# Copying a transposed tile out of PSUM in runs: which side of the copy hops

## The chip, the cores and the metric

The kernel runs on one core of one Trainium2 chip. The metric is device time in microseconds (us) of one execution; the kernel before takes 200.59 us (median of three executions, 200.13 to 200.97). The core's engines each work through their own queue in order: TensorE (PE in the profile, with its weight loads listed as PEld), VectorE (DVE), ScalarE (ACT), GpSimd (POOL) and SyncE (SP, which here issues the DMAs). TensorE writes its results into PSUM; ScalarE and VectorE carry them from PSUM into SBUF, from where TensorE reads its operands.

## The reference

The input is a batch of 8 sequences of 2496 rows with 256 features. It is Fourier transformed over rows and over features and the real part kept; the result, 19968 rows of 256, goes through a soft mixture of experts with 32 slots, 8 experts of 4 slots each.

```python
X = np.fft.fft(np.fft.fft(x, axis=1), axis=2).real      # 8 x 2496 x 256, then 19968 x 256
logits = X @ phi                                        # 19968 x 32
d = exp(logits - logits.max(0)); d /= d.sum(0) + 1e-9   # over all rows, for each slot
slot_input = d.T @ X                                    # 32 x 256
h = np.maximum(slot_input[e] @ w1[e], 0); slot_out[e] = h @ w2[e]   # for each expert e
c = exp(logits - logits.max(1)); c /= c.sum(1) + 1e-9   # over the slots, for each row
out = c @ slot_out                                      # 19968 x 256
```

## The kernel before, in words

The transform is never formed as a whole. Only the logits need it, so the projection on the 32 slots is folded into the feature transform, and the row transform, of length 2496 = 64 x 39, is done as a 64-point and a 39-point transform on the much smaller projected data. The batch of 8 is worked as 4 pairs of sequences (index `p`). For each pair the kernel goes through parts, which a written-out list (`ORDER`) strings together; the scheduler of the language then places the instructions of all engines, with the parts of two or three pairs interleaved.

- `part_a` (L210, twice to three times per pair): VectorE adds and subtracts mirrored rows of the loaded `x` into `eo` tiles (L222 to L227); TensorE transposes them 128 x 128 at a time into `pt` (L231); ScalarE copies these to `et` (L232); TensorE multiplies with the folded projection into `z` (L238); ScalarE copies `z` to `zs` (L246).
- `part_t` (L252): TensorE transposes the ten 128 x 128 blocks of `zs` into three PSUM banks (L259), and ScalarE copies them to the SBUF tile `zt` (L262, L266). This is where the change is.
- `part_b` (L268): TensorE does the 64-point transform with `zt` as its weights, three slots at a time, into `a` (L275); ScalarE copies to `o1` (L282).
- `part_c`, `part_e`, `part_d`, `part_u`: the 39-point transform (`lp`, `lm`, L293 and L294) gives the logits `lt`; column maxima (`mx`, `mt`, `nm`), exponentials on ScalarE (`d`, L316), and the inverse transform back (`e` L331, `d` L348, `ds` L356, `u` L373) to the slot inputs.

After the fourth pair come the sum over pairs (`part_m`), the two expert layers (L472, L492) and, for each pair, the row softmax (`part_s`) and the output product (`po`, L576, copied out at L580 and stored). About 22 to 101 us is the stretch in which `part_a`, `part_t` and `part_b` of the pairs lie.

The tile `zt` of a pair has 128 partitions, and in each the shape `[33, 2, 20]`: 33 places (the 32 slots and one of padding), for each place two halves of 20 coefficients. It is fp32, so a place is 40 numbers, 160 bytes. The transposes leave a bank the other way round: `(c s)`, 16 coefficients of 32 slots each, slots next to each other. So the copy also turns slots and coefficients round, and either its reading or its writing has to hop. Two banks of 512 columns go to `zt[:, :, 0, 0:16]` and `zt[:, :, 1, 0:16]`; of the third, two pieces of 128 columns go to the coefficients 16 to 19 of both halves. Per pair that is two copies of 128x512 and two of 128x128, 16 copies in all.

What stands around them in ScalarE's queue matters for the reading. For the second pair (`p` = 1) it is, as the kernel's program has it (each row: line, operation, output<-input, shape; `et_2_0` and `et_2_1` are the last two `et` tiles of that pair, `zs` its last `z` copy):

```order
L262 COPY zt_530<-zt_0_532 128x16x32
L262 COPY zt_530<-zt_1_538 128x16x32
L232 COPY et_2_0_499<-pt_4_0_504 128x512
L232 COPY et_2_1_500<-pt_4_1_510 128x512
L246 COPY zs_294<-z_2_516 128x2x2x64
L232 COPY et_0_0_555<-pt_0_0_560 128x8x64
L266 COPY zt_530<-zt_2_544 128x4x32 x2
L232 COPY et_0_1_556<-pt_0_1_566 128x8x64
```

On TensorE the same stretch is as follows (`pt_4_*` are the last transposes of the pair, `z_2` its last projection, `zt_2` its third bank, `pt_0_*` the first transposes of the next pair):

```order
L231 MATMUL pt_4_0_504<-cs_70,eo_4_293 128x128 x4
L231 MATMUL pt_4_1_510<-cs_70,eo_4_293 128x128 x4
L238 MATMUL z_2_516<-et_2_0_499,wphi 32x128 x4
L238 MATMUL z_2_516<-et_2_1_500,wphi 32x128 x8
L306 MATMUL mt_1_442<-cs_70,mx_1_440 5x120
L311 MATMUL mt_0_415<-cs_70,mex_0_418 120x6
L231 MATMUL pt_0_0_560<-cs_70,eo_0_549 128x128 x4
L259 MATMUL zt_2_544<-cs_70,zs_294 128x128 x2
L231 MATMUL pt_0_1_566<-cs_70,eo_0_549 128x128 x4
L275 MATMUL a_0_687<-cs_72,zt_530 120x128 x4
```

So `z_2` waits for the `et` copies, which stand behind the two copies of L262, and `a` waits for the copies of L266.

Of the kernel before, what the change touches and what calls it, by code (L numbers as in the profile page):

```python
# [17 lines left out]
NSLOT = 32  # L18
# [98 lines left out]
def _build(nc, tc, xh, phih, w1h, w2h, cins, where, out, out0):  # L117
    from contextlib import ExitStack, nullcontext

    v, sc, pe = nc.vector, nc.scalar, nc.tensor  # L120
    ctx = ExitStack()
    with ctx:
# [12 lines left out]
        def sa(shape, name, dt=F32):  # L135
            return sb.tile(shape, dt, name=name, tag="sa", bufs=2)
# [7 lines left out]
        def bank(name, dt=F32):  # L144
            return pp.tile([128, 512], dt, name=name, tag="ps")
# [39 lines left out]
        ps = bank("psphi")  # L185
# [22 lines left out]
        zs, zt, o1, dpm, esb, dsb = {}, {}, {}, {}, {}, {}  # L208
# [43 lines left out]
        def part_t(p):  # L252
            zt[p] = sa([128, GS * NG, 2, NKC], f"zt{p}")
            nc.gpsimd.memset(zt[p][:, NSLOT:], 0.0)
            for b, units in enumerate(([(0, q) for q in range(4)], [(1, q) for q in range(4)], [(0, 4), (1, 4)])):
                ps = bank(f"zt{p}_{b}")
                for i, (h, q) in enumerate(units):
                    u, nq = q // 2, 2 if q < 4 else 1
                    pe.transpose(ps[:, i * 128 : i * 128 + 128], zs[p][:, 4 * u + nq * h + q % 2], ident)  # L259
                if b < 2:  # L260
                    dst = zt[p][:, :NSLOT, b, 0:16].rearrange("p s c -> p c s")
                    sc.copy(dst, ps.rearrange("p (c s) -> p c s", s=NSLOT))  # L262
                else:
                    for h in range(2):
                        dst = zt[p][:, :NSLOT, h, 16:20].rearrange("p s c -> p c s")
                        sc.copy(dst, ps[:, h * 128 : h * 128 + 128].rearrange("p (c s) -> p c s", s=NSLOT))  # L266

        def part_b(p):  # L268
            o1[p] = sa([120, 2, NG, NA], f"o1{p}")
# [323 lines left out]
        def after(f, *a):  # L593
# [5 lines left out]

        parts = {  # L600
            "a": part_a, "t": lambda p, _: part_t(p), "b": lambda p, _: part_b(p), "c": part_c,
            "e": part_e, "d": part_d, "u": lambda p, _: part_u(p), "w": lambda *_: load_w(),
            "m": lambda *_: part_m(), "l": lambda i, _: part_l(i), "v": lambda i, _: part_v(i),
# [54 lines left out]
```

## Time and profile before

| | |
|---|---|
| median of three executions | 200.59 us (200.13 to 200.97) |
| the profiled execution | 201.22 us, of it the span shown in the profile 199.4 us |
| TensorE busy | 174.7 us (88% of the span) |
| ScalarE busy | 132.4 us (66%) |
| VectorE busy | 131.8 us (66%) |
| L262, copies of 128x512 | 8, mean 1202 ns, 8.7 us busy |
| L266, copies of 128x128 | 8, mean 453 ns, 2.7 us busy |
| mean granted TensorE clock | 0.979 |

Times in the profile are microseconds from the start of the span unless marked ns. Two neighbouring instructions on an engine may overlap a little, so a group's busy time can be less than its count times its mean. An engine's idle time is put down to what ended it; idle time of an engine on which nothing waits costs nothing. The view of stretches gives, for each stretch, the busy time of each engine with the number of instructions that began in it, then the TensorE clock that was granted (1.00 is full speed), the share of DMA and the GB/s moved.

### The profile page before, as it was taken

How to read it: one execution, taken by the hardware profiler on the slowest of the kernel's cores; microseconds unless marked ns; L12 is line 12 of the kernel's file. 1: busy time of each engine (PE TensorE's matmuls, PEld its weight loads, DVE VectorE, ACT ScalarE, POOL GpSimd, SP SyncE). 2: the span in 40 equal slices, each digit the busy share in tenths (PEclk: the TensorE clock that was granted, in tenths of full speed). 3: DMA queues.
4: the chain of work that ended last, by engine and by line, in shares of the span. 5: the costliest groups of instructions: out<-in, count | busy, mean ns of one | idle time of the engine just before them, and what ended most of it. 6: DMA issues, size and time to landing. Idle time of an engine off the chain costs nothing.

```text
span 199.4 us, 4290 instructions
## 1 busy us (share of the span) xinstructions
PE 174.7 (88%) x1690; PEld 125.6 (63%) x1690; DVE 131.8 (66%) x238; ACT 132.4 (66%) x277; POOL 24.6 (12%) x27
## 2 busy tenths in 40 slices
PE   0499889969999999989999989999999999989900
PEld 0375575549666877556865859346788877768700
DVE  0599856989993991742357624796677888976700
ACT  2135775579876795687856963763867988896610
POOL 0000000000000000000000100767101357320000
PEclk9999999997999999999999999999999999999995
DMA  5999999998880499600393687991099999799996
GB/s 183 409 427 410 422 420 420 419 391 291 301 363 21 112 358 424 263 0 0 111 283 138 205 326 234 364 404 58 2 378 355 419 409 389 306 421 363 430 426 214
DMA packets 10707, 59.17 MB, mean 297 GB/s; under 512 B 1344, under 2 KB 1728, under 8 KB 5696
## 3 DMA queue, kind: packets, MB, share of 16 engines
q1 hardware_dynamic: 10688, 58.91, 76.0%
q8 instruction: 13, 0.21, 0.4%
q14 instruction: 6, 0.05, 0.1%
HBM read 38.46 MB, written 20.45 MB: 295 GB/s over the span
## 4 chain that ended last, share of the span: by engine, by line
PE 75%; ACT 10%; DMA 2%; DVE 2%; issue 2%; POOL 2%; SPq 0%; ACTq 0%; DVEq 0%; POOLq 0%
PE po L576 17%; PE pt L231 9%; PE z L238 7%; PE a L275 6%; PE e L331 6%; PE u L373 5%; PE d L348 4%; PE h L472 4%; PE so L492 3%; PE lp L293 3%; PE lm L294 3%; PE cT L529 2%; DMA x<-xh 2%; ACT zt L262 2%; PE lT L569 2%
## 5 line engine op out<-in xcount | busy, mean ns | idle before, releaser
L576 PE MATMUL po<-rh,lTs 128*128 128x512 f32 x160 | 42.4, 405 | 1.5 <-ACT lTs L570 0.7
L231 PE MATMUL pt<-cs,eo 128*128 128x128 f32 x160 | 26.9, 300 | 8.9 <-DVE eo L226 7.9
L576 PEld LDWEIGHTS po<-rh,lTs 128*128 128x128 f32 x160 | 28.1, 188 | 8.5 <-ACT o L580 1.8
L232 ACT COPY et<-pt 128x512 f32<-128x512 f32 x40 | 23.1, 592 | 13.8 <-PE pt L231 13.2
L580 DVE COPY o<-po 128x512 f32<-128x512 f32 (+1 forms) x40 | 26.9, 686 | 7.9 <-PE po L576 7.0
L231 PEld LDWEIGHTS pt<-cs,eo 128*128 128x128 f32 x160 | 19.9, 153 | 15.9 <-DVE eo L226 7.9
L580 ACT COPY o<-po 128x512 f32<-128x512 f32 x40 | 23.2, 595 | 7.3 <-PE po L576 7.1
L224 DVE TENSOR_TENSOR x<-x 128x1024 f32<-128x1024 f32 x16 | 19.5, 1217 | 3.0 <-DMA x<-xh 3.0
L238 PE MATMUL z<-et,wphi 128*32 128x256 f32 (+1 forms) x288 | 19.0, 371 | 1.9 <-ACT et L232 1.8
L544 POOL TENSOR_TENSOR c<-c,cm 128x640 f32<-128x640 f32 x8 | 11.8, 1489 | 28.0 <-DVE cm L543 27.0
L316 ACT ACTIVATE d<-lt,nm 120x128 f32<-120x128 f32 x44 | 13.6, 390 | 1.9 <-DVE nm L313 1.8
L226 DVE TENSOR_TENSOR eo<-x 128x512 f32<-128x512 f32 x20 | 13.6, 682 | 0.6 <-PE u L373 0.3
L238 PEld LDWEIGHTS z<-et,wphi 128*32 128x32 f32 x288 | 7.8, 113 | 9.4 <-ACT et L232 4.2
L227 DVE TENSOR_TENSOR eo<-x 128x512 f32<-128x512 f32 x20 | 13.6, 680 | 0.0
L331 PE MATMUL e<-cs,dpm 120*64 120x120 f32 x176 | 13.5, 273 | 0.0
L331 PEld LDWEIGHTS e<-cs,dpm 120*64 120x64 f32 x176 | 10.7, 136 | 3.5 <-issue 2.4
L356 ACT COPY ds<-d 64x320 f32<-64x320 f32 x24 | 10.0, 421 | 4.2 <-PE d L348 3.5
L275 PE MATMUL a<-cs,zt 128*120 128x128 f32 x88 | 12.2, 292 | 0.4 <-ACT zt L266 0.3
L275 PEld LDWEIGHTS a<-cs,zt 128*120 128x120 f32 x88 | 11.1, 196 | 1.9 <-ACT zt L266 1.3
L549 POOL TENSOR_TENSOR c<-c,cm 128x640 f32<-128x640 f32 x8 | 11.0, 1391 | 10.0 <-DVE cm L548 5.5
L570 ACT CAST lTs<-lT 128x512 fp32r<-128x512 f32 x20 | 11.5, 599 | 0.9 <-PE lT L569 0.9
L373 PE MATMUL u<-eo,ds 128*32 128x129 f32 x320 | 11.6, 275 | 0.0
(99 smaller groups left out, 251.4 us busy)
## 6 DMA issues: line engine op xcount, KB each, us to landing
x<-xh SPq DMA_DIRECT2D x16, 1024.0 KB, 11.3
out<-o SPq DMA_DIRECT2D x15, 1024.0 KB, 5.6
w<-w1h SPq DMA_DIRECT2D x6, 1024.0 KB, 8.6
w<-w2h SPq DMA_DIRECT2D x12, 512.0 KB, 6.0
x<-xh SPq DMA_DIRECT2D x4, 896.0 KB, 10.3
out<-o SPq DMA_DIRECT2D x4, 768.0 KB, 6.0
w<-w1h SPq DMA_DIRECT2D x4, 512.0 KB, 5.2
w<-w2h SPq DMA_DIRECT2D x2, 1024.0 KB, 8.0
```

The lines of the kernel that those rows point to most:

```text
L224: v.tensor_tensor(x[:, 0:4], x[:, 0:4], x[:, 4:8], op=ALU.add)
L226: v.tensor_tensor(e[:, :, 0:128], x[:, 0:4, 0:128], x[:, 0:4, 128:256], op=ALU.add)
L227: v.tensor_tensor(e[:, :, 128:256], x[:, 0:4, 0:128], x[:, 0:4, 128:256], op=ALU.subtract)
L231: pe.transpose(b[:, g * 128 : g * 128 + 128], e[:, g, k * 128 : k * 128 + 128], ident)
L232: sc.copy(tr[k][:, :, :, qi, :], b.rearrange("p (g h a) -> p g h a", g=4, h=2))
L238: pe.matmul(z[32 * g : 32 * g + 32, o : o + n], wphi[:, w, :], tr[k][:, g].rearrange("p h q a -> p (h q a)"), start=i != 1, stop=i != 0, t ...
L275: pe.matmul(ps[:120, i * 128 : i * 128 + 128], zt[p][:, GS * g : GS * g + GS].rearrange("p s h c -> p (s h c)"), C("wa"), start=True, stop ...
L316: sc.activation(d[:, g], L[:, g], AF.Exp, bias=nm[:, g : g + 1], scale=1.0)
L331: pe.matmul(ps[64 * k : 64 * k + 64, 120 * i : 120 * i + 120], dpm[p, hf][:, k, 3 * j + i, :], C(name), start=True, stop=True, tile_positi ...
L373: last = pe.matmul(ub[32 * g : 32 * g + 32, 0:129], dsb[p][:, k, c, :], e[:, 0:129] if k == 0 else e[:, 127:256], start=cc == 0, stop=cc == 9,
L576: pe.matmul(po, lT[:, i, :], rh[j].rearrange("p k d -> p (k d)"), start=j == 0, stop=j == 1,)
L580: (v.tensor_copy if n_ev[0] % 2 else sc.copy)(ot[:np_, 2 * i : 2 * i + 2, :].rearrange("p k d -> p (k d)"), po[:np_])
```

## The change

Both sides of the copies of L262 and L266 are described the other way round. Before, the copy goes through the numbers coefficient by coefficient: it reads PSUM in one piece and writes each number 160 bytes after the one before. Afterwards it goes place by place: it reads numbers that lie 32 apart in PSUM (128 bytes), and writes 16 numbers next to each other (64 bytes; 4 numbers, 16 bytes, in the smaller copies), then hops 160 bytes to the next place. The same numbers go to the same addresses, in as many instructions.

```diff
                 if b < 2:
-                    dst = zt[p][:, :NSLOT, b, 0:16].rearrange("p s c -> p c s")
-                    sc.copy(dst, ps.rearrange("p (c s) -> p c s", s=NSLOT))
+                    sc.copy(zt[p][:, :NSLOT, b, 0:16], ps.rearrange("p (c s) -> p s c", s=NSLOT))
                 else:
                     for h in range(2):
-                        dst = zt[p][:, :NSLOT, h, 16:20].rearrange("p s c -> p c s")
-                        sc.copy(dst, ps[:, h * 128 : h * 128 + 128].rearrange("p (c s) -> p c s", s=NSLOT))
+                        sc.copy(zt[p][:, :NSLOT, h, 16:20], ps[:, h * 128 : h * 128 + 128].rearrange("p (c s) -> p s c", s=NSLOT))
```

No engine's order of instructions differs; only the shapes of these copies do. In ScalarE's queue the rows shown above now read as follows (lines at and below the edit have moved up by one or two):

```order
L261 COPY zt_530<-zt_0_532 128x32x16
L261 COPY zt_530<-zt_1_538 128x32x16
L232 COPY et_2_0_499<-pt_4_0_504 128x512
L232 COPY et_2_1_500<-pt_4_1_510 128x512
L246 COPY zs_294<-z_2_516 128x2x2x64
L232 COPY et_0_0_555<-pt_0_0_560 128x8x64
L264 COPY zt_530<-zt_2_544 128x32x4 x2
L232 COPY et_0_1_556<-pt_0_1_566 128x8x64
```

The inner count of the copies went from 32 places to 16 or 4 coefficients; what stands before and behind them is the same.

## The prediction

> **What bounds the kernel now.** First the page: busy times, and the shares of the chain that ended last.
>
> ```profile
> PE 174.7 (88%) x1690; PEld 125.6 (63%) x1690; DVE 131.8 (66%) x238; ACT 132.4 (66%) x277; POOL 24.6 (12%) x27
> PE 75%; ACT 10%; DMA 2%; DVE 2%; issue 2%; POOL 2%; SPq 0%; ACTq 0%; DVEq 0%; POOLq 0%
> ```
>
> TensorE (PE) sets the end; 10% of the chain, 20 us, is ScalarE (ACT). A faster ScalarE copy is worth only what TensorE waits for it. So next: the copies of ScalarE by shape, for what one costs (count | busy us, mean ns of one | idle before).
>
> ```profile
> L262 ACT COPY zt<-zt 128x512 f32<-128x512 f32 x8 | 8.7, 1202 | 0.6 <-PE zt L259 0.6
> L232 ACT COPY et<-pt 128x512 f32<-128x512 f32 x40 | 23.1, 592 | 13.8 <-PE pt L231 13.2
> L266 ACT COPY zt<-zt 128x128 f32<-128x128 f32 x8 | 2.7, 453 | 0.1
> L382 ACT COPY usb<-u 128x129 f32<-128x129 f32 x3 | 0.8, 257 | 0.5 <-PE u L373 0.5
> L356 ACT COPY ds<-d 64x320 f32<-64x320 f32 x24 | 10.0, 421 | 4.2 <-PE d L348 3.5 <-DVE ds L356 0.5
> L295 ACT COPY lt<-lp 120x320 f32<-120x320 f32 x4 | 1.8, 452 | 3.1 <-PE lp L293 3.1
> L534 ACT COPY c<-cT 128x480 f32<-128x480 f32 x8 | 4.4, 565 | 3.8 <-PE cT L529 3.8
> ```
>
> L262 takes twice as long as L232, which moves as many numbers; L266 takes 1.8 times L382.
>
> Then the timeline of both engines where the four pairs meet these copies (start, us, engine line; in brackets the idle time before and what ended it). The first pair:
>
> ```profile
> 22.85 2.17 ACT L262 COPY zt<-zt 128x512 f32<-128x512 f32 x2
> 24.77 0.45 ACT L246 COPY zs<-z 128x256 f32<-128x256 f32 x1
> 25.75 0.66 ACT L266 COPY zt<-zt 128x128 f32<-128x128 f32 x2
> 22.64 1.01 PE L238 MATMUL z<-et,wphi 128*32 128x128 f32 x24
> 25.28 0.44 PE L259 MATMUL zt<-cs,zs 128*128 128x128 f32 x2 [1.04 <-ACT zs L246]
> 25.55 0.60 PE L231 MATMUL pt<-cs,eo 128*128 128x128 f32 x4
> 26.46 2.73 PE L275 MATMUL a<-cs,zt 128*120 128x128 f32 x22 [0.31 <-ACT zt L266]
> ```
>
> z was done at 22.64 + 1.01 = 23.65, but its copy stood behind the two of L262 until 24.77, and TensorE stood still for 1.04 us, then 0.31 us for L266. The second pair:
>
> ```profile
> 39.62 2.16 ACT L262 COPY zt<-zt 128x512 f32<-128x512 f32 x2 [0.58 <-PE zt L259]
> 41.55 1.14 ACT L232 COPY et<-pt 128x512 f32<-128x512 f32 x2
> 40.24 0.38 PE L231 MATMUL pt<-cs,eo 128*128 128x128 f32 x2
> 42.26 1.13 PE L238 MATMUL z<-et,wphi 128*32 128x128 f32 x24 [1.64 <-ACT et L232]
> ```
>
> Here the et copies queue behind L262, and TensorE is idle for 1.64 us from 40.62. This gap has a second price, in the view of stretches (PE busy with its count, PEld, DVE, ACT, POOL, then the granted clock, DMA share, GB/s), cut in pieces of 3.41 us:
>
> ```profile
> 23.84:27.25 3.41, 2.06 (x17) 1.58 (x16) 2.16 (x4) 2.95 (x7) 0.00 (x0) 1.00 1.00 413
> 27.25:30.66 3.41, 3.41 (x29) 3.09 (x28) 1.69 (x3) 2.55 (x5) 0.13 (x1) 1.00 1.00 417
> 40.90:44.32 3.42, 2.00 (x31) 1.41 (x32) 2.92 (x6) 2.16 (x4) 0.00 (x0) 0.97 0.99 380
> 44.32:47.73 3.41, 3.40 (x17) 2.99 (x16) 3.37 (x6) 3.13 (x10) 0.00 (x0) 0.53 0.85 284
> 47.73:51.14 3.41, 3.41 (x29) 2.71 (x31) 3.02 (x5) 2.85 (x8) 0.13 (x1) 1.00 0.89 329
> ```
>
> Right behind the piece with the gap (2.00 us busy) the clock is 0.53 for one piece, and 17 matmuls begin in it where 29 do in the pieces like it. The first pair's piece, 2.06 us busy, was followed by no drop: we are at the edge.
>
> **The change part by part.** It removes and adds no instruction and moves none; 16 copies of ScalarE get another shape.
>
> *The 128x512 copies.* The new form hops on the reading side (128 bytes) and writes runs of 64. L356 reads numbers 80 bytes apart and writes runs of 16, and takes 421 ns for 320 against 452 for L295, which reads straight. L534 reads 160 bytes apart and writes runs of 12, at 565 ns for 480, between 452 at 320 and 592 at 512. Neither pays for hops in PSUM, so I take L232's 592 ns, saving 610 ns each. The ends: 421 x 512 / 320 is more than 592, so nothing shows a copy below it; above, 1202 ns (no gain) if a hop of 128 bytes reads as slowly as one of 160 writes. I take the low end because both hopping readers lie there.
>
> [...]
>
> *The 128x128 copies.* Their runs are only 4 numbers, which no row shows. The ends are L382's 257 ns and today's 453; I take 257, since a run of 12 (L534) costs nothing visible. With a pair overlapping, 0.66 us becomes about 0.40.
>
> *What a pair of copies frees.* A pair of L262 holds ScalarE from 22.85 to 24.77, 1.92 us. Pairs of copies like L232 show how closely these follow each other:
>
> ```profile
> 49.09 1.08 ACT L232 COPY et<-pt 128x512 f32<-128x512 f32 x2
> ```
>
> 1.08 less 0.59 for the last is 0.49 from start to start, so two take 0.98 and what follows may begin 0.94 us earlier. ScalarE's busy time falls by some 16 x 0.3 = 5 us; most of it is idle time elsewhere.
>
> *First pair.* The copy of zs may start at 23.83 (z is done at 23.65), TensorE's transposes at 24.34 instead of 25.28: 0.94. Then L266 starts 0.94 earlier and ends 0.26 sooner yet, at 25.18; TensorE is through L231 at 25.2 and starts a at about 25.25 instead of 26.46. **1.2 us.**
>
> *Second pair.* et starts at 40.6 instead of 41.55 (TensorE's pt is done at 40.62, so it is there in time), z at 41.3. **0.95 us.**
>
> *Third and fourth pair.*
>
> ```profile
> 64.88 2.19 ACT L262 COPY zt<-zt 128x512 f32<-128x512 f32 x2
> 66.82 0.46 ACT L246 COPY zs<-z 128x256 f32<-128x256 f32 x1
> 68.83 0.38 PE L259 MATMUL zt<-cs,zs 128*128 128x128 f32 x2
> 90.48 0.85 PE L238 MATMUL z<-et,wphi 128*32 128x128 f32 x20
> 90.55 0.79 ACT L340 COPY e<-e 128x360 f32<-128x360 f32 x2
> 91.39 1.34 PE L348 MATMUL d<-e,cs 128*128 128x320 f32 x4
> ```
>
> In the third, zs is done at 67.28 and TensorE wants it at 68.83, having been busy with other matmuls: nothing. In the fourth the e copies behind L262 release L348 at 91.39, but TensorE is in z until 90.48 + 0.85 = 91.33: nothing, and perhaps 0.1 at the a behind L266. What hides these is the interleaved work of other pairs; without it each would be another 0.95.
>
> *The half-speed piece.* With the second gap 0.95 us shorter, its piece is busy for about 2.95 us instead of 2.00, well above the 2.06 that went without a drop. Then the 12 missing matmuls fit: 12 / 29 x 3.41 = 1.4 us. Not all arrives, because VectorE (DVE) can follow only so far. Its waits there:
>
> ```profile
> 43.62 0.27 DVE L308 TENSOR_REDUCE mall<-mt 5x3 f32<-5x120 f32 x1 [0.50 <-PE mt L306]
> 48.12 0.56 DVE L318 TENSOR_TENSOR dpm<-d 120x384 f32<-120x384 f32 x1 [0.43 <-ACT d L316]
> 54.31 0.49 DVE L319 TENSOR_TENSOR dpm<-d 120x320 f32<-120x320 f32 x1
> 57.09 0.62 PE L331 MATMUL e<-cs,dpm 120*64 120x120 f32 x4
> 62.22 0.48 DVE L356 COPY ds<-d 64x320 f32<-64x320 f32 x1 [2.37 <-PE d L348]
> ```
>
> It has 0.50 + 0.43 = 0.93 us of waits to give up before 55, so its dpm, done at 54.80, comes no earlier than 53.87. TensorE needs it at 57.09 and can come forward by 3.2, against 1.2 + 0.95 + 1.4 = 3.55. By 62.22 VectorE waits for TensorE again, and later work follows. So of the 1.4 I count **1.0**.
>
> [...]
>
> *Sum.* 1.2 + 0.95 + 0.1 + 1.0 = 3.25 us off the profiled execution's 201.22 (span 199.4, 1.8 around it), 198.0. That execution lies 0.6 above the median, 200.59. Whether the runs behind the median had the half-speed piece isn't known: if so, 200.59 - 3.25 = 197.3; if not, 200.59 - 2.25 = 198.3. I take **197.9 us**.
>
> **The rivals.**
> - *Queue time alone.* The clock drops anyway (another gap falls into one window) or hadn't dropped in the runs behind the median: 2.25 us, 198.3 to 199.0. For it: at 2.00 and 2.06 us the same kernel did and didn't drop. Against: no gap of that size is left.
> - *VectorE holds the gain.* It is busy 3.37 of 3.41 us in the half-speed piece. If TensorE hangs on it more closely than I read (through the eo tiles for pt, say), 0.93 us is all that comes through: 199.7. Against: the 2.3 us between dpm and its use.
> - *The copy doesn't get cheaper.* A number read 128 bytes from the last costs what one written 160 bytes away does, and the copy stays at 1.2 us: 200.6. Against: L356 and L534. For: neither hops by a power of two. [...]
> - *Slower.* The same place, worse: the hopping read costs more than the hopping write did. From a start-to-start of 0.96 us upward every 0.1 costs 0.2 at the first, second and fourth pair, and the first pair's piece, 0.06 us from the edge, drops its clock too, 1.4. At 1.2 us: 6 x 0.24 + 1.4 = 2.8, 203.4. Nothing in the profile speaks for it beyond the stride that no row has.
>
> **How the numbers follow.** Chances: my forecast 0.45, queue time alone 0.25, VectorE 0.14, no cheaper 0.09, slower 0.07. The range runs from 196.8 (the 197.3 above with another 0.5 us from the 0.4 not counted and the two later pairs) to 200.3, which leaves out the slower and most of the no-cheaper case. 0.5%, 1.0 us, is what the timing can tell apart, so faster means below 199.6: the first two cases less 0.02, and 0.04 of the third, 0.72; within it 0.21; slower 0.07.
>
> **What would show it.** The 128x512 copies at about 590 ns and the 128x128 ones at about 260; the first pair's a at about 25.2; TensorE's wait for et in the second pair at 0.7 us or less; 29 matmuls and clock 1.00 after it; third and fourth pair with no shorter gaps on TensorE. Copies that stay above 900 ns would make it wrong at its root; copies at 590 ns with a time above 199.6, in the step from queue to TensorE.

## The result and the profile after

The changed kernel takes 197.71 us (median), against 200.36 us for the kernel before in the same comparison: a ratio of 0.9865, 95% interval 0.9835 to 0.9895, or 2.65 us less. A second comparison gave 197.48 against 200.70, 0.9835 (0.9809 to 0.9862). One of the six executions of the changed kernel took 903.28 us, for a reason that nothing here shows; the median counts it, the ratio does not, and the other five lie between 197.51 and 197.97. The profiled execution took 197.51 us with a span of 195.7, where the one before took 201.22 with 199.4.

First, the copies by shape in the changed kernel (count | busy us, mean ns of one | idle before); the lines of the edit are now L261 and L264.

```profile
L261 ACT COPY zt<-zt 128x512 f32<-128x512 f32 x8 | 4.3, 596 | 0.6 <-PE zt L259 0.6
L264 ACT COPY zt<-zt 128x128 f32<-128x128 f32 x8 | 1.8, 280 | 0.0
L232 ACT COPY et<-pt 128x512 f32<-128x512 f32 x40 | 23.0, 594 | 13.8 <-PE pt L231 13.2
```

The large copies went from 1202 to 596 ns and now cost what L232 costs, 594, the small ones from 453 to 280. Reading PSUM in hops of 128 bytes costs ScalarE nothing that can be seen here. ScalarE as a whole went from 132.4 to 127.4 us busy, 5.0 us less; the time fell by about half of that in the median.

The first pair in the timeline of ScalarE and TensorE (start, us, engine line, then idle time before):

```profile
22.72 1.08 ACT L261 COPY zt<-zt 128x512 f32<-128x512 f32 x2
23.67 0.41 ACT L246 COPY zs<-z 128x256 f32<-128x256 f32 x1
24.68 0.44 ACT L264 COPY zt<-zt 128x128 f32<-128x128 f32 x2
22.51 1.01 PE L238 MATMUL z<-et,wphi 128*32 128x128 f32 x24
24.13 0.44 PE L259 MATMUL zt<-cs,zs 128*128 128x128 f32 x2
25.17 2.72 PE L273 MATMUL a<-cs,zt 128*120 128x128 f32 x22 [0.17 <-ACT zt L264]
```

The copy of zs starts at 23.67, 0.15 us after its z is done (22.51 + 1.01) where it had been 1.12, and TensorE's wait of 1.04 us is gone; a starts at 25.17 instead of 26.46. The second pair:

```profile
38.34 1.07 ACT L261 COPY zt<-zt 128x512 f32<-128x512 f32 x2 [0.58 <-PE zt L259]
39.30 1.10 ACT L232 COPY et<-pt 128x512 f32<-128x512 f32 x2
39.95 1.14 PE L238 MATMUL z<-et,wphi 128*32 128x128 f32 x24 [0.62 <-ACT et L232]
43.09 2.01 PE L273 MATMUL a<-cs,zt 128*120 128x128 f32 x16 [0.41 <-ACT zt L264]
```

TensorE's wait for et fell from 1.64 to 0.62 us. There is also a wait that was not there before: a waits 0.41 us for the small copies.

Now the pieces of 3.41 us around the gap (PE busy with its count, PEld, DVE, ACT, POOL, granted clock, DMA share, GB/s). The clock of the profiled execution before fell at 44.13 and rose at 47.54, 0.19 us ahead of where the prediction cut its pieces. In its clock records full clock begins at 16.82, and the clock changes 27.31, 3.41 and 146.77 us from one to the next, 8, 1 and 43 times 3.41; after the change it begins at 16.96 and changes once, 174.08 us or 51 times 3.41 later. So the pieces are laid out in steps of 3.41 us from the beginning of these records. Before:

```profile
40.71:44.13 3.42, 1.81 (x30) 1.22 (x31) 2.92 (x7) 2.35 (x5) 0.00 (x0) 1.00 1.01 387
44.13:47.54 3.41, 3.40 (x17) 2.99 (x16) 3.41 (x6) 2.94 (x9) 0.00 (x0) 0.50 0.89 303
```

After the change:

```profile
37.44:40.85 3.41, 2.39 (x37) 1.82 (x36) 3.41 (x7) 2.37 (x5) 0.00 (x0) 1.00 0.99 408
40.85:44.27 3.42, 3.01 (x34) 2.47 (x23) 3.42 (x6) 2.53 (x8) 0.00 (x0) 1.00 1.02 418
44.27:47.68 3.41, 3.41 (x29) 2.65 (x31) 3.41 (x7) 3.31 (x9) 0.13 (x1) 1.00 0.98 371
```

The gap, which now ends at 39.95, lies in the first of these, with 2.39 us of work. The clock stays at 1.00, and in the third, at nearly the same time of the span as the half-speed piece before, 29 matmuls begin where there were 17. Following the same matmul through both traces shows where the 3.7 us of the span came from:

| matmul of TensorE | start before | start after | earlier by |
|---|---|---|---|
| the first transposes, pt | 7.89 | 7.65 | 0.24 |
| first pair, a | 26.46 | 25.17 | 1.29 |
| second pair, last z | 42.26 | 39.95 | 2.31 |
| second pair, a | 45.67 | 43.09 | 2.58 |
| second pair, first lp | 50.18 | 46.79 | 3.39 |
| third pair, a | 71.01 | 67.61 | 3.40 |
| fourth-pair stretch, d | 91.39 | 87.87 | 3.52 |
| fourth pair, a | 93.82 | 90.16 | 3.66 |
| first expert layer, h | 125.33 | 121.66 | 3.67 |
| last po | 189.19 | 185.56 | 3.63 |

Just ahead of the first pair's copies (22.85 to 22.72) the two executions were 0.13 us apart, which has nothing to do with the change. So: 1.16 at the first pair, 1.02 at the second pair's gap, 1.08 between that gap and lp, where the clock had been halved, nothing from 47 us to the fourth pair, 0.26 around the fourth pair, and nothing given back in the 100 us behind it.

### The profile page after: what moved, and what is told of

Read it like the earlier page. It is cut to its first block, busy times and chain, and to the rows that moved or that the text cites. A ratio compares the mean times of both kernels' runs of the same rounds, so it can differ in the third digit from the quotient of the medians.

```text
span 195.7 us, 4290 instructions
## 1 busy us (share of the span) xinstructions
PE 173.1 (88%) x1690; PEld 124.3 (63%) x1690; DVE 131.5 (67%) x238; ACT 127.4 (65%) x277; POOL 24.6 (13%) x27
## 4 chain that ended last, share of the span: by engine, by line
PE 79%; ACT 8%; DVE 3%; DMA 2%; POOL 2%; issue 2%; SPq 0%; ACTq 0%; DVEq 0%; POOLq 0%
PE po L574 17%; PE pt L231 10%; PE z L238 8%; PE e L329 7%; PE a L273 6%; PE u L371 6%; PE d L346 4%; PE h L470 4%; PE so L490 4%; PE lp L291 3%; PE lm L292 3%; PE cT L527 3%; DMA x<-xh 2%; PE lT L567 2%; POOL c L542 2%; ACT et L232 2%
## 5 line engine op out<-in xcount | busy, mean ns | idle before, releaser
L231 PE MATMUL pt<-cs,eo 128*128 128x128 f32 x160 | 26.4, 297 | 8.7 <-DVE eo L226 7.6
L232 ACT COPY et<-pt 128x512 f32<-128x512 f32 x40 | 23.0, 594 | 13.8 <-PE pt L231 13.2
L273 PE MATMUL a<-cs,zt 128*120 128x128 f32 x88 | 11.4, 279 | 0.6 <-ACT zt L264 0.6
L273 PEld LDWEIGHTS a<-cs,zt 128*120 128x120 f32 x88 | 10.2, 183 | 1.9 <-ACT zt L264 1.3
```

Of the source, the lines that this page charges most:

```text
L231: pe.transpose(b[:, g * 128 : g * 128 + 128], e[:, g, k * 128 : k * 128 + 128], ident)
L232: sc.copy(tr[k][:, :, :, qi, :], b.rearrange("p (g h a) -> p g h a", g=4, h=2))
L273: pe.matmul(ps[:120, i * 128 : i * 128 + 128], zt[p][:, GS * g : GS * g + GS].rearrange("p s h c -> p (s h c)"), C("wa"), start=True, stop ...
```

## Experiments

The theory: time is saved only where TensorE waits for these copies, 1.2 us at the first pair and 1.0 at the second, and a further 1 us or so where the second gap had halved the clock. The rival: every copy is worth the same, a quarter of the gain for each pair.

### One pair at a time

Three kernels in one comparison, each with the new shape for some pairs:

```diff
-                if b < 2:
+                if b < 2 and p == 0:      # first kernel; p == 1 in the second, p >= 2 in the third
                     sc.copy(zt[p][:, :NSLOT, b, 0:16], ps.rearrange("p (c s) -> p s c", s=NSLOT))
+                elif b < 2:
+                    sc.copy(zt[p][:, :NSLOT, b, 0:16].rearrange("p s c -> p c s"), ps.rearrange("p (c s) -> p c s", s=NSLOT))
...
```

(the 128x128 copies likewise).

> Only the first pair's four copies get the new shape. My theory: 1.2 us (the zs copy 0.94 earlier, the last small copy another 0.26), so about 199.2; the second pair's idle gap on TensorE stays at about 1.6 us. Rival, every copy worth the same: a quarter of the 2.65 us, 0.66, about 199.7.

> Only the second pair's four copies get the new shape. My theory: TensorE's wait for et falls from 1.64 to 0.65 us, 0.95 to 1.0 us, and the half-speed piece, where there was one, goes: together 1.0 to 2.1 us, about 198.8, with a mean clock of 0.985 or more in all executions. The first pair keeps its 1.04 us gap. Rival, every copy worth the same: 0.66 us, about 199.7, and the clock as often at 0.979 as before.

> Only the third and fourth pairs' copies get the new shape. My theory: nothing at the third, 0.1 to 0.26 us at the fourth, so 200.1 to 200.3, and the clock as often at 0.979 as before. Rival, every copy worth the same: half of 2.65 us, 1.3, about 199.0.

| new shape for | median us | ratio to before | 95% interval | gain us |
|---|---|---|---|---|
| first pair | 199.23 | 0.9945 | 0.9926 to 0.9964 | 1.1 |
| second pair | 199.03 | 0.9936 | 0.9912 to 0.9960 | 1.3 |
| third and fourth | 199.92 | 0.9991 | 0.9966 to 1.0017 | 0.2 |

(Gain: one less the ratio, times the 200.31 us median of before in this comparison.) The three add up to 2.6 us, the whole gain. A quarter each, 0.66 us, would be a ratio of 0.9967, outside the intervals of the first two, and 1.3 us for the last two pairs, 0.9934, is outside theirs. What TensorE waited for, first in the kernel with the first pair, then with the second (engine line waited for: us in total, times, longest):

```profile
PE z L238 <- ACT et L232: 1.8, 2, 1.6
PE zt L259 <- ACT zs L246: 0.3, 1, 0.3
```

```profile
PE zt L259 <- ACT zs L246: 1.4, 2, 1.0
PE z L238 <- ACT et L232: 0.8, 2, 0.6
```

Each pair's copies close that pair's wait and leave the other's alone.

### The second pair's gap, whole and half

Two kernels beside those of the next section: in one the second pair alone keeps the old shape, in the other only the first 128x512 copy of the second pair does.

```diff
-                if b < 2:
+                if b < 2 and p != 1:              # whole gap
+                if b < 2 and (p != 1 or b == 1):  # half the gap; 128x128 copies all new
...
```

> All copies in the new shape except those of the second pair, so the second gap comes back and the first stays closed. My theory: 1.0 us slower than the changed kernel from the queue, and up to 1.1 more in executions where the clock drops behind the gap: 198.7 to 199.8. Rival, every copy worth the same: 0.66 us slower, about 198.4, without a dropped clock.

> As the changed kernel, but of the second pair's two 128x512 copies the first keeps the old shape, so that the gap there is half as much longer. My theory: TensorE's wait for et is about 1.1 us and the time 0.5 us above the changed kernel's 197.7, about 198.2, and the clock does not drop, as the piece around the gap is still busy for about 2.5 us of 3.41. Rival, the clock falls with any longer gap: 1.5 us slower.

All but the second pair: 199.11 us, ratio 0.9922 (0.9891 to 0.9952). Half the gap: 197.79, 0.9857 (0.9825 to 0.9888). The whole gap costs 1.1 or 1.7 us, by this ratio against 0.9865 or 0.9835 of the changed kernel, within the first forecast of 1.0 to 2.1; 198.4 of the rival lies below all its executions (198.71 to 199.50), and four of the six have a mean clock of 0.979 or less. In the kernel with half the gap TensorE's wait for et was 1.1 us, as forecast:

```profile
PE z L238 <- ACT et L232: 1.3, 2, 1.1
```

but its time is not separable from the changed kernel's, where 0.5 us more had been expected; the intervals allow either. The rival's 1.5 us more is out, and no execution has a mean clock below 0.982.

### The clock behind the gap

> The kernel before itself, timed so that the granted clock of every execution is seen. My theory: some executions hold the 3.4 us piece at half speed (mean clock about 0.979, time about 201) and some do not (0.985 or more, about 1.1 us less), since the gap of the second pair lies just at the edge. Rival: the clock is the same in all executions, and the spread of 199.6 to 201.0 has nothing to do with it.

> The changed kernel again, beside the fused one on the same chip, and with the clock of every execution. My theory: 197.7, a mean clock of 0.982 or more in all executions (no half-speed piece in the middle); against executions of the kernel before at 0.985 or more it is 2.0 to 2.1 us faster, against those at 0.979 or less 3.4 to 3.6 us. Rival: executions at 0.979 or less turn up here too, and the gap of the second pair had nothing to do with them.

The kernel before against itself gave 1.0008 (0.9978 to 1.0038). Its executions in the comparisons that show a clock for each, 68 in all, fall into three groups by mean granted clock:

| mean clock | executions | mean us | range |
|---|---|---|---|
| 0.977 to 0.979 | 24 | 201.2 | 200.8 to 201.6 |
| 0.982 | 20 | 200.5 | 200.1 to 201.0 |
| 0.985 to 0.987 | 24 | 199.8 | 199.3 to 200.3 |

The changed kernel's ten executions that the ratios count lie at 0.984 to 0.988, at 197.7 and 197.5 us on average in the two comparisons. Against the last group that is 2.1 to 2.3 us less, against the first 3.5 to 3.8.

The mean clock isn't a measure of the drop alone: it also counts the end of the span, where TensorE has no work left (in the profile of before the clock is 0.50 from 194.3 us on). Of the 13 profiles of this case the four at 0.979 or less have the half-speed piece behind the second gap, and the nine at 0.982 or more, of which one is at 0.982, don't. No profile of the kernel before fell into the middle group, and what sets it apart is not shown.

An execution at 0.979 or less turned up in 12 of 30 executions of the kernels that keep the second pair's old copies (first pair only, last two only, all but the second), and in none of 45 of those in which at least one of that pair's two large copies is new. The lowest clock among the 45 is 0.980, in four executions, none of them more than 0.2 us above its kernel's median. So it is the second gap, at its full length, that lets the clock fall. The pieces around it, in the repeated kernel before, with the last two pairs alone, and with half the gap:

```profile
40.50:43.92 3.42, 1.73 (x31) 0.91 (x29) 2.97 (x5) 2.66 (x5) 0.00 (x0) 1.00 1.04 388
43.92:47.33 3.41, 3.40 (x16) 2.98 (x16) 3.35 (x7) 2.19 (x6) 0.00 (x0) 0.50 0.75 296
```

```profile
39.74:43.16 3.42, 1.72 (x31) 1.02 (x29) 3.22 (x5) 2.80 (x4) 0.00 (x0) 1.00 1.01 420
43.16:46.57 3.41, 2.77 (x26) 2.40 (x23) 3.10 (x7) 2.68 (x8) 0.00 (x0) 1.00 0.91 346
```

```profile
37.50:40.91 3.41, 1.95 (x18) 1.47 (x21) 3.41 (x6) 2.83 (x5) 0.00 (x0) 1.00 1.01 416
```

The same 1.64 us gap, with 1.73 and 1.72 us of work in its piece, halved the clock in one execution and not in the other. So the busy time of the piece doesn't decide by itself, and what does stays open.

What the drop costs can be read from the distance between the second pair's last z and its first lp, with that pair's old copies: 7.92 us in the profile of before (42.26 to 50.18) and 7.87 in its repeat (42.62 to 50.49), both with the drop, against 6.98 with the last two pairs alone (42.11 to 49.09), where the clock stayed up. That is 0.9 us and not the 1.4 that the matmul count gives, because at full speed TensorE reaches a before the small copies are done and waits:

```profile
42.11 1.13 PE L238 MATMUL z<-et,wphi 128*32 128x128 f32 x24 [1.64 <-ACT et L232]
45.46 2.01 PE L282 MATMUL a<-cs,zt 128*120 128x128 f32 x16 [0.64 <-ACT zt L273]
```

So the drop explains some 0.9 of the 1.4 us between the first and the last group; where the rest comes from is not shown.

The pieces lie differently in each execution: by the clock records of the traces, full clock came at 16.8 us in the profile of before and at 14.6 in that of the kernel with the first pair alone, and the clock fell at 44.13 and 41.88. The 14.6 explains an oddity in part. With the first pair alone, executions at 0.979 or less were no slower (199.3) than those at 0.982 to 0.984 (199.2). In its profile the half-speed piece is there:

```profile
38.46:41.88 3.42, 1.72 (x30) 0.89 (x29) 2.91 (x6) 2.66 (x5) 0.00 (x0) 1.00 1.00 414
41.88:45.29 3.41, 3.40 (x16) 3.00 (x16) 3.41 (x8) 2.31 (x8) 0.00 (x0) 0.50 1.03 421
```

but full clock at the start came early, its first 24 matmuls of z taking 1.87 us instead of the 2.79 in the profile of before, and the 0.92 us between them nearly cancels the 0.9 of the drop. One profile each is too few to show that this holds for all of them.

### Large copies alone, and one small copy for two

```diff
-                        sc.copy(zt[p][:, :NSLOT, h, 16:20], ps[:, h * 128 : h * 128 + 128].rearrange("p (c s) -> p s c", s=NSLOT))
+                        sc.copy(zt[p][:, :NSLOT, h, 16:20].rearrange("p s c -> p c s"), ps[:, h * 128 : h * 128 + 128].rearrange("p (c s) -> p c s", s=NSLOT))   # large alone
```

```diff
-                    for h in range(2):
-                        sc.copy(zt[p][:, :NSLOT, h, 16:20], ps[:, h * 128 : h * 128 + 128].rearrange("p (c s) -> p s c", s=NSLOT))
+                    sc.copy(zt[p][:, :NSLOT, :, 16:20], ps[:, :256].rearrange("p (h c s) -> p s h c", h=2, s=NSLOT))   # one for two
```

> The 128x512 copies in the new shape, the 128x128 ones in the old. My theory: first pair's a 0.2 us later and second pair's a 0.2 us later than in the changed kernel, the half-speed piece gone: about 198.1 to 198.2, 0.4 above the changed kernel. Rival, time in proportion to the busy time saved (8 x 0.61 us of 6.2 in all): 0.6 above, 198.3; rival two, the small copies are hidden everywhere: 197.7.

> As the changed kernel, and the two 128x128 copies of a pair made one instruction of 128x256 (the same numbers to the same places). A copy of 128x256 in a straight form took 0.41 us in the kernel before, the pair 0.44 us in the changed one. My theory: up to 0.05 us at the first and second pair, 197.6, not to be told apart. Rival: if a pair's second copy overlaps the first no longer but waits for its semaphores, more than 0.2 us at each of them: 197.3 or less.

> The kernel with one 128x256 copy in the place of the two 128x128 copies of a pair. Its profile shows TensorE's wait for that copy gone at the first pair (0.17 us before) and 0.4 us at the second as before. My theory: 0.1 to 0.2 us faster than the changed kernel, which this measurement can't tell apart. Rival: 0.3 us or more faster, as the ratios of the two calls (0.9836 against 0.9865) would have it.

Large copies alone: 198.05 us, ratio 0.9859 (0.9823 to 0.9895), so nearly all of the gain is theirs; the 0.4 us expected of the small ones can't be told from nothing by the times. By the profile, with the old small copies TensorE's waits for them were 1.0 us in all, against 0.6 in the changed kernel:

```profile
PE a L282 <- ACT zt L273: 1.0, 2, 0.6
```

One copy for two took 380 ns against 440 for the overlapping pair. It gave 197.52 us, 0.9836 (0.9805 to 0.9868), and beside the changed kernel on one chip 196.85 against 197.48, 0.9811 (0.9782 to 0.9841) against 0.9835 (0.9809 to 0.9862). In its profiles TensorE's wait at the first pair is gone and the second's is 0.35 us instead of 0.41:

```profile
PE a L275 <- ACT zt L263: 0.3, 1, 0.3
```

That is 0.2 us of waits less. On the one chip the medians lie 0.6 us apart, more than these waits and on the side of the rival, but the intervals overlap, so a faster version is suggested and not shown, and where more than 0.2 us would come from is open.

### How long a run has to be

The 128x512 copies were written in runs of 16, 8, 4, 2 and single numbers within one kernel (one execution), the 128x128 copies of the first and third pair in runs of 2, and those of the second and fourth as one 128x256 copy each (the cut shows the large copies alone):

```diff
-                    sc.copy(zt[p][:, :NSLOT, b, 0:16], ps.rearrange("p (c s) -> p s c", s=NSLOT))
+                    sc.copy(   # i=r for the length of the run
+                        zt[p][:, :NSLOT, b, 0:16].rearrange("p s (o i) -> p o s i", i=r),
+                        ps.rearrange("p (o i s) -> p o s i", s=NSLOT, i=r),
+                    )
```

> The changed kernel with the 128x512 copies written in runs of different lengths, one look for the length of a copy: first pair runs of 8 and 4, second pair 2 and 16, third 2 and 4, fourth 8 and 1; the 128x128 copies in runs of 2 in the first and third pair, and fused to one 128x256 with runs of 4 in the second and fourth. [...] Theory two, every hop costs: 512 hops cost 610 ns, so 1.2 ns each: about 670 for runs of 8, 745 for 4, 900 for 2, 1200 for 1. The time itself should lie between 197.5 and 199.

```profile
L273 ACT COPY zt<-zt 128x512 f32<-128x512 f32 x1 | 0.6, 592 | 0.0
L267 ACT COPY zt<-zt 128x512 f32<-128x512 f32 x1 | 0.6, 593 | 0.0
L269 ACT COPY zt<-zt 128x512 f32<-128x512 f32 x1 | 0.6, 606 | 0.0
L271 ACT COPY zt<-zt 128x512 f32<-128x512 f32 x1 | 0.7, 659 | 0.6 <-PE zt L259 0.6
L281 ACT COPY zt<-zt 128x512 f32<-128x512 f32 x1 | 1.2, 1172 | 0.0
L290 ACT COPY zt<-zt 128x128 f32<-128x128 f32 x4 | 0.9, 305 | 0.0
```

From the top: runs of 16, 8, 4, 2 and 1, and the small copies in runs of 2. A second copy of each of the middle lengths gave 592 (8), 603 (4) and 669 (2). So the step is between 1 and 2: a run of 2 costs 70 ns over 512 numbers, a run of 4 some 12, and 8 nothing. A price for each hop, theory two, would have made runs of 2 cost 900 ns and is out. The small copies in runs of 2 took 305 ns, in the changed kernel, with runs of 4, 280. What makes single numbers cost twice as much, 1172 ns against 592, is not shown. The kernel took 197.1 us, the kernel before beside it 199.6.

## Why the prediction was right

**The result.** 197.9 was forecast with a range of 196.8 to 200.3; 197.71 was measured, and 197.48 in the second comparison.

**The price of a copy.** Right at the large ones: 592 forecast, 596 measured, and the hopping read free against the 594 of L232, as L356 and L534 had let expect. The rivals in which the copy does not get cheaper, or dearer, are out. The small ones were taken at 257 ns and measured 280; the pair at 0.44 us instead of 0.40.

**First pair.** 1.2 us forecast, 1.16 in the trace, 1.1 alone. (The end of L266 in the working should read 25.21 instead of 25.18, which changes nothing.) **Second pair.** 0.95 forecast, 1.02 in the trace.

**Third and fourth.** Nothing at the third, as forecast: its a, at 71.01 and 67.61, is 3.40 earlier like the matmuls ahead of it. At the fourth 0.1 was forecast and 0.26 measured: the e copies do release d sooner, by 0.12, and a follows L264 by another 0.14.

**The half-speed piece.** 1.0 of its 1.4 was counted and 1.08 arrived, but not for the reason given: that the size came out is luck. The step that failed is the sentence that VectorE has 0.93 us of waits to give up and that TensorE can therefore come forward by no more than 3.2 us. VectorE waits for TensorE further up too, 2.49 us for lm up to 31.47, and there it moved forward with the first pair: the same instruction began at 30.18, 1.29 earlier. With the 0.93 that makes 2.2 of the 2.4 by which its dpm moved in the second pair, before at 48.12 and 54.31 to 54.80, and now:

```profile
45.75 0.54 DVE L316 TENSOR_TENSOR dpm<-d 120x384 f32<-120x384 f32 x1
51.84 0.47 DVE L317 TENSOR_TENSOR dpm<-d 120x320 f32<-120x320 f32 x1
53.70 0.62 PE L329 MATMUL e<-cs,dpm 120*64 120x120 f32 x4
```

It came 2.4 to 2.5 us earlier, without a wait, and done at 52.31 it is 1.4 us ahead of its use at 53.70, so it holds nothing. What kept part of the 1.4 back is the wait of a for the small copies, 0.41 us, which the slow clock had covered: before, ScalarE was done with them at 45.62 and TensorE only at 45.65. With the last two pairs alone, where the clock stayed up and these copies are old, the same wait was 0.64. The rival of a gain held by VectorE falls with the same rows.

Two readings of the pieces were off as well. Cut where the clock changed, the piece with the gap before holds 1.81 us of work, not 2.00, so 2.06 without a drop was less near an edge than it looked. And the shorter gap did not leave its piece at 2.95 us: the gap fell into the piece ahead, with 2.39. That the drop goes was right all the same.

**Queue time alone against the whole.** Both occur. Executions of the kernel before at the highest clock (199.8) lost 2.1 to 2.3 us, for which 2.25 had been worked out, and those with the dropped clock (201.2) lost 3.5 to 3.8, for which it had been 3.25; of the drop itself the traces show 0.9. The median of 200.4 lies between, in the middle group, and what its executions lost beyond the queue time isn't known. So a value between the two sums was a fair choice, but that it came within 0.2 us of the measured time is partly luck.

**The expectations.** Missed were half the gap (198.2 expected, 197.79 measured); the clock with the second pair alone (0.985 or more expected in all executions, 0.980 to 0.985 measured); one small copy for two (0.1 to 0.2 us faster expected, 0.6 measured, not separable); and the time of the kernel with several run lengths (197.5 to 199 expected, 197.09 measured). With the last two pairs alone 199.92 was a little below the 200.1 to 200.3 expected, within its interval. Of the kernel before two groups were expected, 1.1 us apart, and three came, 1.4 from first to last. That the clock would turn on the busy time of the piece was also too simple, as 1.73 and 1.72 us with and without a drop show.

## What to carry to other kernels

A copy that turns two dimensions round has a choice of side. On ScalarE it paid here to let the reading side in PSUM hop and to write runs of at least four fp32 numbers into SBUF: with single numbers the 128x512 copy took 1172 to 1202 ns, about double, and with runs of 4 to 16 it took 592 to 606, within 3% of the 592 to 594 of a straight copy. What that is worth is read from what queues behind the copy and from who waits there: of 16 copies made faster, the eight of the first two pairs gave nearly all of the gain (1.1 and 1.3 us alone, the other eight 0.2), since interleaved work of other pairs covered the rest. And a gap of 1.64 us on TensorE cost a second time in some executions, by halving its clock, from 1.00 to 0.50, for 3.41 us: some 0.9 us here.

## What the runs showed of the hardware beyond that

The clock of TensorE halved, from 1.00 to 0.50, in some executions and not in others at the same gap of 1.64 us: it fell behind pieces of 3.41 us with 1.72, 1.73, 1.75 and 1.81 us of work, and did not behind another with 1.72. Behind pieces with 1.95 (half the gap) and 2.06 (the first pair's) it did not fall either. In the kernel before 24 of 68 executions lay in the slowest of three groups by mean clock, 1.4 us above the fastest, which is most of the spread of its times (199.3 to 201.6); the ten executions of the changed kernel that the ratios count lay within 197.2 to 198.0, closer together, though they are fewer.
